# Leaving out sixteen spare matrix products behind the early heads of an attention and MoE kernel

## The chip, the cores and the metric

The kernel runs on one core of one Trainium2 chip. The metric is the device time of one execution in microseconds (us). The kernel before took 1030.9 us as the median of 3 runs (1030.06 to 1033.68 us). The trace comes from one profiled execution of 1030.28 us, whose span from the first to the last instruction is 1027.9 us. All durations below are from that execution.

## The reference

Three layers are computed one after the other, in float32:

```python
scores = scale * q @ k.T                         # 4 batches x 8 heads, 576 x 576, head_dim 64
cum    = cumsum(max(s, 0))
scores = where(causal, -1e9, scores + min(-(cum_i - cum_j), 0))
x      = softmax(scores) @ v                     # 2304 tokens x 512
xn     = x / sqrt(mean(x*x) + 1e-6) * rms_g
x      = (silu(xn @ w_gate) * (xn @ w_val)) @ w_out      # 512 -> 1536 -> 512
out    = (silu(x @ w2_gate) * (x @ w2_val)) @ w2_out
```

## The kernel before

**Arithmetic.** TensorE works here on float32 values that are split in two halves, a rounded value H and a rest L. A product of two float32 matrices is taken as three products, H·H, H·L and L·H. So every weight block that comes from memory ("raw") is first converted: ScalarE reads it (L479, into `cvy`), VectorE merges it (L481), ScalarE or GpSimd writes H (L486, L487), VectorE or GpSimd subtracts and writes L (L490). One block is half of one of the 12 column groups f of the gate and value weights.

**Stages.** First come 22 matrix passes on zeros (L559). Then eight "early quads": the first 128 rows of all 32 heads, four heads to a quad. A quad has scores on TensorE (L924, L927), a masked minimum on VectorE (L932), the exponential on ScalarE (L937), a transpose on TensorE (L949), a copy of it by ScalarE or VectorE (L953, L954), a product with the values (L958) and a copy into x (L968, L969). After quads 0 to 3, and again after quads 4 to 7, the rows are normalised: ScalarE squares x (L992), TensorE sums (L999), VectorE forms a factor (L1052 to L1083) with one power on GpSimd in between (L1086), TensorE turns it round (L1095) and spreads it (L1106), VectorE scales x (L1110), ScalarE and VectorE or GpSimd write its halves xH and xL (L1113, L1115). With that the first MoE layer of these 512 rows can start (L1126): for the first five groups f (`HALVES = 5`) in two parts of 256 rows, one for each of the two normalisations. Its results pass through tanh on ScalarE (L1133) and two VectorE operations (L1135, L1138) into one of three buffers `t`, and SyncE stores them (L1167). Beside it the 32 full heads are attended (L650 to L883: loads, the halves kHH, kLL, qst and vst, scores L714 and L839, transposes L784, products L796), with the MoE products as work to fill in. The second half of the program multiplies by w_out (L1488) and computes the second MoE layer (L1669, L1542, L1745).

**What sets the order.** Nothing of this order is written by hand. Every operation is entered in a plan with an engine (or a choice of engines), an assumed duration, what it reads and writes, and a priority `pri`; smaller is sooner. A list scheduler then runs through assumed time: whenever an engine is free it takes the ready operation with the smallest `pri`, and a choice of engines falls to the one that is free first. The order in which operations were taken is the order in which each engine executes them, one after the other, waiting where data is late. A changed duration or operation thus moves everything that is planned later. Four PSUM banks (`mo`) are handed to whoever needs one next.

**The place of the change.** Behind the eighth early quad a loop over `IDLE` enters products that nobody reads (L1256 to L1260): each takes an `mo` bank of its own, multiplies the 128x128 identity `ident` with itself, may start when quad 3 has its exponentials ("early 3"), and has priority 1.0e9, behind all other work. They are taken only when no other product is ready by the plan's clock.

```python
for _ in range(IDLE):
    spare = mo_bank()
    op(PE, 216, lambda en, spare=spare: en.matmul(
        spare()[:, :P], ident(), ident(), start=True, stop=True),
       r=[ident, "early 3"], w=[spare], pri=1.0e9)
```

Of the kernel before, what the change touches and what calls it, by code (L numbers as in the profile page):

```python
# [326 lines left out]
TINY = 70  # L327

HALVES = 5
IDLE = 16  # L330


@with_exitstack
def tile_kernel(
# [63 lines left out]
    def mo_bank():  # L398

        return shared("ps", "mo", 4, [P, 512], F32)  # L400
# [854 lines left out]
    last_setup()  # L1255
    for _ in range(IDLE):  # L1256
        spare = mo_bank()
# [699 lines left out]
```

## Time and profile before

| | |
|---|---|
| median of 3 runs | 1030.9 us |
| profiled execution | 1030.28 us |
| its span | 1027.9 us |
| TensorE (PE) busy | 1019.9 us, 99% |
| VectorE (DVE) busy | 764.2 us, 74% |
| ScalarE (ACT) busy | 632.7 us, 62% |
| GpSimd (POOL) busy | 266.5 us, 26% |

The page calls the engines PE (matrix products; PEld is their weight load), DVE, ACT, POOL and SP. A line number stands for a line of the kernel. A row of a timeline has the start, the time, the engine, the line, the operation with what it writes and reads, and in brackets how long the engine had been idle and what ended that. The ends of products are modelled and overlap the next start; how long a product occupies TensorE is read from the distance of two starts. Each planned product of the identity shows as two records.

### The profile page before, as it was taken

The page shows a single profiled execution, that of the slowest core. Times are in us where ns is not written, and L with a number is a line of the kernel's source. Part 1 is how long each engine was busy: PE and PEld are TensorE (multiplying, and loading weights), DVE is VectorE, ACT ScalarE, POOL GpSimd, SP SyncE. Part 2 cuts the span into 40 slices and gives each one's busy share as a digit, 9 for nine tenths or more (in the row PEclk, how much of TensorE's full clock was granted, in tenths as well). Part 3 has the DMA queues.
Part 4 walks back from the last instruction along what each step waited for, and adds up shares of the span by engine and source line. Part 5 has one row for each costly group of instructions (what it writes and reads, how often), then busy time and mean ns, then how long its engine had stood idle before and what let it go on. Part 6 is the DMA issues. An engine that isn't in the chain of part 4 may idle for free.

```text
span 1027.9 us, 17596 instructions
## 1 busy us (share of the span) xinstructions
PE 1019.9 (99%) x5546; PEld 901.9 (88%) x5546; DVE 764.2 (74%) x1748; ACT 632.7 (62%) x1315; POOL 266.5 (26%) x357
## 2 busy tenths in 40 slices
PE   9999999999999999999999999999999999999998
PEld 9998889999999999899888889888888888788888
DVE  7999887677778796568889896566768667866562
ACT  6889877766687465334567675555665545665653
POOL 3678754444444440100000000212312122200000
PEclk9999999999999999999999999999999999999999
DMA  9874533343445674479888652765757766888772
GB/s 348 266 250 144 182 115 120 123 139 104 121 130 152 215 248 149 147 247 303 273 283 279 210 156 98 243 213 200 259 192 244 267 226 231 305 271 254 215 240 93
DMA packets 122718, 212.07 MB, mean 206 GB/s; under 512 B 19009, under 2 KB 46913, under 8 KB 122625
## 3 DMA queue, kind: packets, MB, share of 16 engines
q1 hardware_dynamic: 122288, 210.61, 62.7%
q8 instruction: 44, 0.72, 0.3%
q14 instruction: 50, 0.40, 0.1%
q10 hardware_dynamic: 336, 0.34, 0.1%
HBM read 146.33 MB, written 64.56 MB: 205 GB/s over the span
## 4 chain that ended last, share of the span: by engine, by line
PE 90%; DVE 4%; DMA 3%; ACT 1%; issue 1%; POOL 0%; SPq 0%; DVEq 0%; ACTq 0%; POOLq 0%
PE mo L1126 23%; PE mo L1669 11%; PE mo L1488 9%; PE sps L1669 9%; PE sps L1488 6%; PE tp L1488 6%; PE tp L796 4%; PE tp L784 3%; PE sps L714 3%; PE mo L1745 3%; PE mo L1542 2%; PE tp L1669 1%; PE sps L1126 1%; PE tp L1126 1%; DMA h_d<-t 1%; PE sps L839 1%
## 5 line engine op out<-in xcount | busy, mean ns | idle before, releaser
L1126 PE MATMUL mo<-xL,H 128*128 128x448 f32 (+2 forms) x472 | 169.3, 359 | 0.7 <-DVE xL L1115 0.7
L1126 PE MATMUL mo<-xH,L 128*128 128x448 f32 (+2 forms) x472 | 169.7, 360 | 0.2 <-DVE L L490 0.2
L1126 PE MATMUL mo<-xH,H 128*128 128x448 f32 (+2 forms) x472 | 168.9, 359 | 0.0
L751 ACT ACTIVATE sc<-sc,col 128x256 f32<-128x256 f32 (+2 forms) x96 | 60.6, 631 | 59.6 <-DVE col L740 58.9
L1126 PEld LDWEIGHTS mo<-xL,H 128*128 128x128 f32 x472 | 88.8, 188 | 6.0 <-DVE xL L1115 0.9
L1126 PEld LDWEIGHTS mo<-xH,L 128*128 128x128 f32 x472 | 88.8, 188 | 5.6 <-DVE L L490 0.4
L1408 DVE TENSOR_TENSOR hL<-hh,hH 128x512 fp32r<-128x512 f32 (+1 forms) x96 | 63.7, 667 | 39.5 <-ACT hH L1405 38.8
L1126 PEld LDWEIGHTS mo<-xH,H 128*128 128x128 f32 x472 | 88.7, 188 | 4.9
L1405 ACT ACTIVATE hH<-hh 128x512 fp32r<-128x512 f32 (+1 forms) x96 | 57.6, 603 | 50.7 <-DVE hL L1408 21.1
L1488 PE MATMUL mo<-hH,wo 128*128 128x512 f32 x208 | 68.5, 389 | 0.0
L789 DVE TENSOR_TENSOR pTB<-tp,pTB 128x512 fp32r<-128x512 f32 (+1 forms) x96 | 56.3, 597 | 14.0 <-ACT pTB L787 13.4
L1675 ACT ACTIVATE u<-sps 128x512 f32<-128x512 f32 x48 | 28.5, 594 | 54.8 <-PE sps L1669 54.7
L787 ACT ACTIVATE pTB<-tp 128x512 fp32r<-128x512 f32 (+1 forms) x96 | 48.5, 517 | 13.5 <-PE tp L784 12.8
L796 PEld LDWEIGHTS tp<-pTB,vst 128*128 128x128 f32 x320 | 52.9, 188 | 4.3 <-DVE pTB L789 0.8
L796 PE MATMUL tp<-pTB,vst 128*128 128x448 f32 (+3 forms) x320 | 55.3, 313 | 0.1
L784 PE MATMUL tp<-ident,sc 128*128 128x128 f32 x320 | 51.3, 273 | 0.1
L1684 ACT ACTIVATE u<-u 128x512 f32<-128x512 f32 x48 | 29.5, 631 | 33.4 <-DVE u L1679 33.4
L1632 POOL TENSOR_TENSOR tmp<-x,x 128x512 f32<-128x512 f32 x2 | 2.6, 1298 | 171.7 <-ACT r L1405 171.7
L1488 PEld LDWEIGHTS mo<-hH,wo 128*128 128x128 f32 x208 | 39.1, 188 | 8.1
L784 PEld LDWEIGHTS tp<-ident,sc 128*128 128x128 f32 x320 | 39.7, 140 | 6.1 <-DVE pTB L789 0.3
L728 POOL TENSOR_SCALAR_AFFINE_SELECT sc<-cb 128x128 f32<-128x128 f32 x96 | 35.2, 381 | 38.0 <-PE tp L784 36.9
L1133 ACT ACTIVATE t<-mo 128x448 f32<-128x448 f32 (+2 forms) x59 | 30.4, 516 | 22.7 <-PE mo L1126 15.5
(318 smaller groups left out, 3023.0 us busy)
## 6 DMA issues: line engine op xcount, KB each, us to landing
raw<-in_w_gv SPq DMA_DIRECT2D x44, 511.8 KB, 5.7
tb<-h_d SPq DMA_DIRECT2D x48, 256.0 KB, 3.6
t<-tb SPq DMA_DIRECT2D x48, 256.0 KB, 3.1
lq<-in_qk SPq DMA_DIRECT2D x32, 288.0 KB, 3.8
cb<-cum_d SPq DMA_DIRECT2D x32, 288.0 KB, 3.7
h<-t SPq DMA_DIRECT2D x32, 256.0 KB, 3.4
h<-h_d SPq DMA_DIRECT2D x24, 256.0 KB, 3.0
row0B<-u SPq DMA_DIRECT2D x24, 256.0 KB, 3.3
```

Source lines behind the costliest of these rows:

```text
L714: op(PE, c_mm(n), lambda en, pt=pt, at=at, c=c, n=n, z=z, kk=kk: en.matmul(pt()[:, :n], qst[j]()[:, at:at + 128], kk()[:, c:c + n], start= ...
L728: op(POOL, 165 + 0.85 * m, lambda en: en.affine_select(out=sc()[:m, o:o + m], in_=cb()[:m, o:o + m], pattern=[[-1, m]], base=0, compare_op ...
L751: op(ACT, c_act(o + m, 2) + 35, lambda en: en.activation(sc()[:m, :o + m], sc()[:m, :o + m], ACTF.Exp, scale=-1.0, bias=col()[:m, 0, t:t + 1],
L784: op(PE, C_TR, lambda en, pt=pt, a=a, kb=kb, t=t: en.transpose(pt()[:, a * P:a * P + P], self.sc[t]()[:, kb * P:kb * P + P], ident()), r=[ ...
L787: op(ACT, c_act(n), lambda en, pt=pt, c=c: en.activation(place(H, c), source(pt, c), ACTF.Copy), r=[pt], w=[(H, c)], pri=pri)
L789: op(DVE, c_tt(n), lambda en, pt=pt, c=c: en.tensor_tensor(out=place(L, c), in0=source(pt, c), in1=f32(place(H, c)), op=ALU.subtract), r=[ ...
L796: op(PE, c_mm(n), lambda en, w=w, z=z, kb=kb, d0=d0, n=n, o=o: en.matmul(po()[:, o:o + n], vst[j]()[:, kb, :], pT[z]()[:, d0:d0 + n], star ...
L1126: op(PE, c_mm(n), lambda en, a=a, x=x, c=c, k=k, i=i: en.matmul(ps()[:, :n], a()[:, c], x(k, lo, n), start=(k == 0 and i == 0), stop=(k == ...
L1405: op(ACT, c_act(n) + 35, lambda en: en.activation(H(), src(), ACTF.Copy), r=[src, *after], w=[H], pri=pri)
L1408: lambda en: en.tensor_tensor(out=L(), in0=src(), in1=f32(H()), op=ALU.subtract),
L1488: op(PE, c_mm(n), lambda en, m=m, w=w, xx=xx, kk=kk, i=i: en.matmul(ps[m]()[:, :n], w(), xx(), start=first and kk == 0 and i == 0, stop=kk ...
L1669: op(PE, c_mm(n), lambda en, w=w, xx=xx, cut=cut, kk=kk, i=i: en.matmul(ps()[:, :n], W[w]()[:, cut], xx(), start=first and kk == 0 and i == 0,
```

## The change

The number of spare products goes from sixteen to none. Nothing else is edited.

```diff
 HALVES = 5
-IDLE = 16
+IDLE = 0
```

The scheduler then sets another order from the first of these products on. On TensorE, behind the score products of the sixth early quad (`sps`; `mo` are the shared banks, `tp` a bank for transposes, `ev` the values, `early` the exponentials turned round), the difference begins so:

```order
 L924 MATMUL sps_400<-eq 128x128
 L927 MATMUL sps_400<-heights 128x128
-L1258 MATMUL mo_424<-ident 128x128
-L1258 MATMUL mo_429<-ident 128x128
 L999 MATMUL mo_368<-half,sq_110 128x2 x2
 L999 MATMUL mo_368<-half,sq_351 128x2 x2
-L958 MATMUL mo_441<-early_112,ev 128x128 x4
-L949 MATMUL tp_457<-ident,sc_407 128x128 x4
```

Two of the sixteen stood ahead of the sums of the first normalisation, and these now follow the scores at once.

On GpSimd, before, from the power of the first normalisation (`rc`, L1086) to that of the second and to the first head's kLL:

```order
L1086 TENSOR_TENSOR rc_453<-rc_453,minus_half 128x2
L1090 TENSOR_SCALAR fenced<-sq_351 128x1
L487 TENSOR_SCALAR H_534<-raw_377 128x512
L487 TENSOR_SCALAR H_534<-raw_395 128x512
L490 TENSOR_TENSOR L_557<-raw_377,H_534 128x512
L490 TENSOR_TENSOR L_557<-raw_395,H_534 128x512
L1115 TENSOR_TENSOR xL_122<-x,xH_123 128x256
L728 AFFINE_SELECT sc_669<-cb_611 128x128
L728 AFFINE_SELECT sc_678<-cb_611 128x128
L490 TENSOR_TENSOR L_698<-raw_468,H_675 128x512
L1086 TENSOR_TENSOR rc_685<-rc_685,minus_half 128x2
L668 TENSOR_TENSOR qst_708<-lq_566,qst_708 64x512
```

and now:

```order
L1086 TENSOR_TENSOR rc_442<-rc_442,minus_half 128x2
L490 TENSOR_TENSOR L_411<-raw_307,H_402 128x512
L1090 TENSOR_SCALAR fenced<-sq_351 128x1
L487 TENSOR_SCALAR H_513<-raw_377 128x512
L622 MEMSET sc_538 128x64
L622 MEMSET sc_540 128x64
L624 MEMSET sc_542 128x64
L624 MEMSET sc_544 128x64
L1115 TENSOR_TENSOR xL_122<-x,xH_123 128x256 x2
L1086 TENSOR_TENSOR rc_629<-rc_629,minus_half 128x2
L1090 TENSOR_SCALAR fenced<-sq_351 128x1
L490 TENSOR_TENSOR L_610<-raw_446,H_599 128x512
```

The second power stood behind five conversions of weights, one half of x and two masks; now one subtraction and one conversion of weights, four small memory fills and two halves of x are ahead of it.

On SyncE's queue, before, the last loads of weights (`raw`) of the second batch, the first stores of the MoE results (`h_d`) and the next head's loads (`lq`, `vl`):

```order
L475 DMA raw_773<-in_w_gv 128x2047
L475 DMA raw_794<-in_w_gv 128x2047
L1167 DMA h_d_70<-t_657 128x256
L652 DMA lq_817<-in_qk 64x512
L475 DMA raw_826<-in_w_gv 128x2047
L1167 DMA h_d_70<-t_717 128x256
L650 DMA lq_817<-in_qk 128x576
L475 DMA raw_870<-in_w_gv 128x2047
L1167 DMA h_d_70<-t_766 128x256
```

and now:

```order
L475 DMA raw_742<-in_w_gv 128x2047
L1167 DMA h_d_70<-t_638 128x256
L475 DMA raw_772<-in_w_gv 128x2047
L475 DMA raw_794<-in_w_gv 128x2047
L1167 DMA h_d_70<-t_682 128x256
L475 DMA raw_825<-in_w_gv 128x2047
L475 DMA raw_846<-in_w_gv 128x2047
L1167 DMA h_d_70<-t_734 128x256
L475 DMA raw_879<-in_w_gv 128x2047
L652 DMA lq_902<-in_qk 64x512
```

The head's load that stood behind the first store now stands behind the third, and two weight loads stand between the stores.

On all engines the two orders are interleaved differently up to the end of the attention and are the same again behind it: on TensorE the last rows that differ are near row 2280 of 4919.

## Rows read from the trace of the kernel before

**Rows 1.** From the page: busy time by engine, granted TensorE clock, chain that ended last.

```profile
PE 1019.9 (99%) x5546; PEld 901.9 (88%) x5546; DVE 764.2 (74%) x1748; ACT 632.7 (62%) x1315; POOL 266.5 (26%) x357
...
PEclk9999999999999999999999999999999999999999
...
PE 90%; DVE 4%; DMA 3%; ACT 1%; issue 1%; POOL 0%; SPq 0%; DVEq 0%; ACTq 0%; POOLq 0%
```

**Rows 2.** Busy time by stretch: length, five engines, granted clock, DMA share, GB/s.

```profile
26.00:32.00 6.00, 6.00 (x55) 5.94 (x55) 4.67 (x21) 5.93 (x19) 3.65 (x5) 1.00 0.95 300
...
54.00:55.00 1.00, 0.50 (x5) 0.30 (x3) 1.00 (x1) 1.00 (x3) 1.00 (x2) 1.00 1.12 367
...
46.00:60.00 14.00, 12.20 (x87) 10.83 (x87) 13.53 (x29) 10.37 (x23) 12.03 (x14) 1.00 0.82 282
...
100.00:200.00 100.00, 100.00 (x585) 90.14 (x584) 77.68 (x259) 76.24 (x184) 56.92 (x87) 1.00 0.46 141
```

**Rows 3.** The spare products' own line: duration min/median/max in ns, first and last start.

```profile
L1258 PE MATMUL mo<-ident x32: 275/275/377, 21.9 to 48.8; 128*128 128x128 f32 x32
```

**Rows 4.** Timeline of PE: the first products, and 28 to 56 us.

```profile
1.04 4.62 PE L559 MATMUL mo<-sq 128*128 128x128 f32 x22 [1.04 <-DVE sq L555]
...
28.37 0.83 PE L1258 MATMUL mo<-ident 128*128 128x128 f32 x6
29.04 0.27 PE L949 MATMUL tp<-ident,sc 128*128 128x128 f32 x1
...
33.24 1.14 PE L958 MATMUL mo<-early,ev 128*128 128x128 f32 x8
34.14 0.36 PE L1126 MATMUL mo<-xH,H 128*128 128x256 f32 x1
...
47.20 0.56 PE L714 MATMUL sps<-kLL,qst 128*128 128x256 f32 x2 [0.51 <-POOL kLL L671]
...
55.25 0.38 PE L1126 MATMUL mo<-xL,H 128*128 128x256 f32 x1 [0.74 <-DVE xL L1115]
```

**Rows 5.** Timeline of ACT: four kinds of work before the first matrix layer, and two waits.

```profile
21.47 0.58 ACT L953 ACTIVATE early<-tp 128x512 f32<-128x512 f32 x1
...
34.42 0.39 ACT L968 ACTIVATE x<-mo 128x256 f32<-128x256 f32 x1 [0.91 <-PE mo L958]
34.70 0.67 ACT L486 ACTIVATE H<-raw 128x512 fp32r<-128x512 f32 x1
...
36.44 0.78 ACT L479 ACTIVATE cvy<-raw 128x512 f16<-128x512 bf16 x1
...
47.69 0.39 ACT L1133 ACTIVATE t<-mo 128x256 f32<-128x256 f32 x1 [2.59 <-DMA h_d<-t]
```

**Rows 6.** Timeline of DVE: the first factor, and two weight merges beside GpSimd.

```profile
30.13 0.17 DVE L1052 TENSOR_SCALAR fac<-totE 128x16 f32<-128x16 f32 x1 [1.09 <-ACT sc L937]
...
37.25 0.69 DVE L481 SCALAR_TENSOR_TENSOR raw<-raw,cvy 128x512 uint32<-128x512 uint32 x1
...
44.51 3.19 DVE L481 SCALAR_TENSOR_TENSOR raw<-raw,cvy 128x512 uint32<-128x512 uint32 x2
```

**Rows 7.** Timeline of POOL: ahead of the second power, and the first head's kLL.

```profile
38.84 1.33 POOL L490 TENSOR_TENSOR L<-raw,H 128x512 fp32r<-128x512 f32 x1 [4.03 <-issue]
40.11 1.18 POOL L1086 TENSOR_TENSOR rc<-rc,minus_half 128x2 f32<-128x2 f32 x1
...
45.29 1.86 POOL L671 TENSOR_TENSOR kLL<-lq,kHH 128x576 fp32r<-128x576 f32 x1
```

**Rows 8.** The DMA queue of SP, and one transfer in the chain of waits.

```profile
33.04 5.17 SPq L475 DMA_DIRECT2D raw<-in_w_gv  x6
39.33 0.33 SPq L1167 DMA_DIRECT2D h_d<-t  x1
47.18 0.48 SPq L652 DMA_DIRECT2D lq<-in_qk  x1
...
39.33 8.28 DMA h_d<-t
```

## The prediction

> **What bounds the kernel now.** I read the page first. TensorE is busy 99% of the span, and it is 90% of the chain that ended last [rows 1]. So the end is the sum of TensorE's work and of the moments in which it has none, and an edit to it can be counted in full only where TensorE's work is late because of other work of its own. Then I read the busy time by stretch: from 100 to 200 us TensorE is busy for all 100 us [rows 2], and the stretches of 100 us up to 1000 look alike. The only larger loss lies early: from 46 to 60 us it is busy for 12.20 of 14 us [rows 2], 1.8 us idle. The spare products lie just there and ahead of it, between 21.9 and 48.8 us [rows 3]. Last I read the timelines of that stretch engine by engine, to see who sets the pace.
>
> **What the products cost.** The sixteen show as 32 records [rows 3]. Six of them start at 28.37 and the next product at 29.04 [rows 4]: 0.67 us, 0.112 us each. All 32 occupy 32 x 0.112 = 3.6 us of TensorE. That is all that can be saved directly. From 26 to 32 us TensorE shows 6.00 of 6 us busy, but ScalarE shows 5.93 of 6 as well [rows 2]; 26 of the 32 records lie between 26.2 and 32.4 us by the timeline, and without them that stretch has only half its work on TensorE. There ScalarE sets the pace: exponentials, copies and weight conversions of the early quads, which the first MoE products need. So the larger part of the 3.6 us is room that TensorE has anyway.
>
> **What comes sooner all the same.** Two things of the new order shorten ScalarE's line. Counted from the order of both programs, between the sixth quad's exponentials and the first half of x, ScalarE loses one copy of transposed exponentials (L953, 0.58 us) to VectorE, has one conversion of weights less there (L479, 0.78 us) and takes one H more (L486, 0.67 us) [rows 5]: 0.58 + 0.78 - 0.67 = 0.7 us less. VectorE's 1.09 us of waiting for the last exponential at 30.13 [rows 6] can shrink by as much. Second, the last values product (L958) starts at 33.24 behind spare products and sums [rows 4], and ScalarE waits 0.91 us for it at 34.42 [rows 5]; now it stands ahead of the sums. The bounds for this stage are 0.7 us (ScalarE's line alone) and 0.7 + 0.91 = 1.6 us (its wait gone too), or nothing where VectorE, which took the copy, becomes late itself. I take 1.3 us, nearer to the upper end, since the wait of 0.91 us ends with a TensorE row that is moved for certain. The MoE products that start at 34.14 [rows 4] should then start near 32.9.
>
> From there to 46 us TensorE is dense in both. What comes then is the hole of 1.8 us. It has named ends: the first head's kLL from GpSimd (0.51 us) and xL of the second normalisation (0.74 us) [rows 4]. Both were late for reasons that the new order touches. The second power ran only behind a subtraction, at 40.11 instead of 38.84 [rows 7]; now it stands ahead of these subtractions. VectorE needed 3.19 us for two merges, where one alone takes 0.69 [rows 6], while GpSimd computed kLL [rows 7]; the scaling of x stood behind them. And SyncE's queue stood still from 39.33 to 47.18 us, its next load waiting until GpSimd had read the buffer at 45.29 + 1.86 = 47.15 [rows 7, 8]; this load now stands behind the third store. Against that, kLL of the first head moves to VectorE, and its scores come later on TensorE. The bounds are the whole 1.8 us gained and as much lost again; I take 0.7 us gained.
>
> **The sum.** 1.3 + 0.7 = 2.0 us less than the profiled execution: 1030.28 - 2.0 = 1028.3 us. (The execution lies 0.6 us under the median of 1030.9; differences are taken from it.) The other 2.3 of the 3.6 us of vacated TensorE time turn into waiting for ScalarE, and so cost nothing and bring nothing. The rest of the reordering, up to the end of the attention, I count at zero: MoE products fill TensorE there [rows 2]. If that cover had a gap, a change of one wait of the size seen at 55.25, 0.74 us [rows 4], would be its price.
>
> [...]
>
> **The rivals.**
>
> *First, all of it is gained.* If the new order closes the hole as well as the products' time, the gain is 3.6 + 1.8 = 5.4 us: 1024.9 us. For it speaks that TensorE sets the end from 75 us on [rows 1, 2] and that all three causes of the hole are touched at once. Against it, ScalarE at 5.93 of 6 us [rows 2], whose work is the same.
>
> [...]
>
> *Third, the stores come too late.* SyncE now has two weight loads between one store of the MoE results and the next. The first store of before, behind six loads, took 8.28 us to land [rows 8], and ScalarE stood 2.59 us at L1133 for the buffer [rows 5]. If the next two stores each hold ScalarE up as long, TensorE lacks weights and banks for 5.2 us; less the 2.0 us gained this is +3.2 us: 1033.5 us. It decides when a store lands more than about 8 us after its issue while the third buffer is full. For it: the loads come without the pause of before. Against it: the first store has five loads ahead instead of six.
>
> *Fourth, nothing.* ScalarE's line is no shorter because VectorE's copy comes late, and the hole keeps its size: 1030.3 us.
>
> **How the numbers follow.** The forecast gets 0.40, all of it gained 0.22, nothing 0.14, the clock 0.12, late stores 0.12. What a measurement can tell from no change is 0.3%, 3.1 us. Faster by more: the first rival and a few parts of the forecast, 0.25. Slower by more: the two slow rivals less the cases in which they cost a little under 3.1 us, 0.19. Within: 0.56. The range goes from 1024.6, just under the first rival, to 1034.0, the clock's price; the forecast's own is 1026.8 to 1030.0.
>
> **What would show it.** In the changed profile the line of the spare products is gone; TensorE shows idle time between 26 and 32 us, some 2 us, and ends of it are ScalarE rows or what they feed; the first MoE product of the dense run starts near 33 us; ScalarE's wait of 0.91 us at L968 is gone; between 46 and 60 us idle time is 1 us or a little more; behind 75 us everything stands 2 us earlier. [...] I am wrong if the dense run starts no earlier than 34, if the hole behind 46 us grows past 2 us, or if TensorE idles later, in the attention, where I counted nothing.

## The result and the profile after

The changed kernel took 1037.27 us (median of 10 runs, 1032.39 to 1041.47) against 1031.07 us for the kernel before, measured beside it: a ratio of 1.0052, 95% interval 1.0037 to 1.0068. One of the ten executions of the kernel before took 1697.28 us; the ratio leaves it out and is taken over all the others, so it is not the quotient of the two medians. The changed kernel is slower by 0.5%, where I forecast a small gain; the time lies outside the range too. The profiled execution took 1037.88 us with a span of 1036.1 us, 8.2 us more than before. At the first product with w_out (L1488), 495.00 us into the span before and 502.89 us now, 7.9 us of it are already there; from 100 to 200 us TensorE is busy for 99.84 of 100 us, against 100.00 before [rows 2]. So most of the loss lies ahead of 100 us. From the page of the changed kernel, granted clock and the chain that ended last:

```profile
PEclk9989999999999999999999999999999999999999
...
PE 74%; DVE 10%; DMA 7%; ACT 4%; issue 3%; SPq 1%; POOL 1%; DVEq 0%; ACTq 0%; POOLq 0%
```

TensorE's share of the chain fell from 90% to 74% and VectorE's rose from 4% to 10% [rows 1]; one slice of the clock, from 52 to 78 us, is below 0.9. Busy time by stretch of the changed kernel (length, PE, PEld, DVE, ACT, POOL, granted clock, DMA share, GB/s):

```profile
0.00:100.00 100.00, 89.75 (x640) 84.41 (x641) 86.33 (x274) 77.72 (x207) 53.44 (x87) 0.95 0.71 242
46.00:60.00 14.00, 9.75 (x59) 9.18 (x60) 13.94 (x22) 8.55 (x17) 9.77 (x14) 0.79 0.37 133
26.00:32.00 6.00, 4.32 (x32) 3.39 (x30) 4.96 (x22) 5.76 (x19) 2.25 (x8) 1.00 0.95 331
60.00:75.00 15.00, 14.60 (x102) 14.21 (x101) 11.98 (x38) 9.89 (x23) 5.45 (x6) 0.86 0.70 219
```

and the same first 100 us of the kernel before:

```profile
0.00:100.00 100.00, 96.92 (x716) 90.93 (x717) 87.73 (x291) 82.56 (x220) 66.42 (x97) 1.00 0.74 251
```

TensorE is idle for 10.25 us instead of 3.08: 7.2 us more. 3.6 us of products are gone, and some of the work ran at half clock (granted 0.50), as the timeline of PE shows:

```profile
30.89 0.78 PE L1106 MATMUL mo<-xH,sel 128*128 128x256 f32 x2 [1.02 <-DVE x L1110]
...
32.27 1.16 PE L958 MATMUL mo<-early,ev 128*128 128x128 f32 x8 [0.37 <-DVE x L1110]
33.27 0.95 PE L999 MATMUL mo<-half,sq 128*128 128x2 f32 x8
34.08 0.37 PE L1126 MATMUL mo<-xL,H 128*128 128x256 f32 x1
...
47.55 0.97 PE L1106 MATMUL mo<-xH,sel 128*128 128x256 f32 x2 [3.02 <-DVE x L1110]
48.32 0.41 PE L1126 MATMUL mo<-xH,H 128*128 128x256 f32 x1
48.53 0.41 PE L1126 MATMUL mo<-xL,H 128*128 128x256 f32 x1
...
58.42 0.90 PE L714 MATMUL sps<-kLL,qst 128*128 128x256 f32 x2 [2.60 <-DVE kLL L671]
```

Two waits of 3.02 and 2.60 us stand where the hole of before had 0.51 and 0.74 us [rows 4]. Behind each the products start 0.213 us apart instead of 0.118, at a granted clock of 0.50 (47.5 to 50 us, and 58.4 to 64 us). 35 products of L1126 ran so (11 from 48.3, 24 from 59.1), 35 x 0.095 = 3.3 us. Idle 7.2 + half clock 3.3 - products 3.6 = 6.9 us of the 7.9; where the last 1.0 us lies these rows do not show.

Both waits are for VectorE. Timelines of DVE and of POOL, changed kernel:

```profile
29.46 0.69 DVE L490 TENSOR_TENSOR L<-raw,H 128x512 fp32r<-128x512 f32 x1 [0.78 <-POOL H L487]
30.07 0.17 DVE L1052 TENSOR_SCALAR fac<-totE 128x16 f32<-128x16 f32 x1
...
43.26 3.50 DVE L490 TENSOR_TENSOR L<-raw,H 128x512 fp32r<-128x512 f32 x2
...
47.02 0.86 DVE L1110 SCALAR_TENSOR_TENSOR x<-x,gcol,mo 128x256 f32<-128x256 f32 x2
...
53.54 1.67 DVE L668 TENSOR_TENSOR qst<-lq,qst 64x512 fp32r<-64x512 f32 x1
55.24 1.79 DVE L481 SCALAR_TENSOR_TENSOR raw<-raw,cvy 128x512 uint32<-128x512 uint32 x1
56.95 1.42 DVE L671 TENSOR_TENSOR kLL<-lq,kHH 128x576 fp32r<-128x576 f32 x1
```

```profile
37.76 1.09 POOL L1086 TENSOR_TENSOR rc<-rc,minus_half 128x2 f32<-128x2 f32 x1 [4.96 <-DVE rc L1060]
...
41.48 4.74 POOL L490 TENSOR_TENSOR L<-raw,H 128x512 fp32r<-128x512 f32 x3
...
53.05 1.61 POOL L668 TENSOR_TENSOR qst<-lq,qst 64x512 fp32r<-64x512 f32 x1
54.74 1.74 POOL L671 TENSOR_TENSOR kLL<-lq,kHH 128x576 fp32r<-128x576 f32 x1
```

VectorE's two L490 take 3.50 us while GpSimd runs three L490, its qst 1.67 us and its merge 1.79 us while GpSimd runs qst and kLL. Alone a merge takes 0.69 us [rows 6], an L490 0.68 (at 34.55 us with GpSimd idle; 0.69 at 29.46 above, beside memory fills of GpSimd). These rows overlap in time, and VectorE's are about two and a half times as long as alone; GpSimd's three L490 take 1.58 us each, against 1.30 at 25.07 us, when VectorE had neither a merge nor a subtraction of halves: in these rows the instructions of both engines are longer while they overlap. What makes them longer, the rows do not show.

Taken over 26 to 75 us, VectorE's merges and subtractions of halves, all marked `port` in the plan ("port work" below), before:

```profile
L481 DVE SCALAR_TENSOR_TENSOR raw<-raw,cvy 128x512 uint32<-128x512 uint32 x16 | 14.5, 935 | 0.0
L490 DVE TENSOR_TENSOR L<-raw,H 128x512 fp32r<-128x512 f32 x4 | 3.5, 875 | 0.2 <-ACT H L486 0.2
L1115 DVE TENSOR_TENSOR xL<-x,xH 128x256 fp32r<-128x256 f32 x4 | 2.8, 728 | 0.0
L671 DVE TENSOR_TENSOR kLL<-lq,kHH 128x576 fp32r<-128x576 f32 x1 | 0.8, 751 | 0.0
L668 DVE TENSOR_TENSOR qst<-lq,qst 64x512 fp32r<-64x512 f32 x1 | 0.7, 685 | 0.0
```

and after:

```profile
L481 DVE SCALAR_TENSOR_TENSOR raw<-raw,cvy 128x512 uint32<-128x512 uint32 x18 | 14.8, 826 | 0.0
L490 DVE TENSOR_TENSOR L<-raw,H 128x512 fp32r<-128x512 f32 x5 | 5.6, 1129 | 1.2 <-POOL H L487 0.8 <-ACT H L486 0.4
L668 DVE TENSOR_TENSOR qst<-lq,qst 64x512 fp32r<-64x512 f32 x2 | 3.3, 1646 | 0.3 <-ACT qst L666 0.2
L1115 DVE TENSOR_TENSOR xL<-x,xH 128x256 fp32r<-128x256 f32 x5 | 3.1, 660 | 0.0
L671 DVE TENSOR_TENSOR kLL<-lq,kHH 128x576 fp32r<-128x576 f32 x1 | 1.4, 1417 | 0.0
```

26 such instructions of 22.3 us became 31 of 28.2 us, on an engine that is busy for 13.94 of 14 us from 46 to 60 us (13.53 before [rows 2]).

### The profile page after: what moved, and what is told of

It is laid out like the page before. It is cut to its first block, busy times and chain, and to the rows that moved or that the text cites. A ratio compares the mean times of both kernels' runs of the same rounds, so it can differ in the third digit from the quotient of the medians.

```text
span 1036.1 us, 17517 instructions
## 1 busy us (share of the span) xinstructions
PE 1020.8 (99%) x5514; PEld 902.1 (87%) x5514; DVE 769.0 (74%) x1748; ACT 633.2 (61%) x1316; POOL 259.0 (25%) x356
## 4 chain that ended last, share of the span: by engine, by line
PE 74%; DVE 10%; DMA 7%; ACT 4%; issue 3%; SPq 1%; POOL 1%; DVEq 0%; ACTq 0%; POOLq 0%
PE mo L1126 19%; PE mo L1669 9%; PE mo L1488 9%; PE sps L1669 7%; PE tp L1488 6%; PE sps L1488 5%; PE tp L796 4%; PE tp L784 3%; PE sps L714 3%; PE mo L1745 2%; DMA cvs<-in_w_o 2%; DMA raw<-in_w_gv 2%; PE mo L1542 2%; PE tp L1669 1%; PE sps L839 1%
## 5 line engine op out<-in xcount | busy, mean ns | idle before, releaser
L1126 PE MATMUL mo<-xL,H 128*128 128x448 f32 (+2 forms) x472 | 170.6, 362 | 0.0
L1126 PE MATMUL mo<-xH,L 128*128 128x448 f32 (+2 forms) x472 | 170.4, 362 | 0.0
L1126 PE MATMUL mo<-xH,H 128*128 128x448 f32 (+2 forms) x472 | 169.9, 361 | 0.0
L1126 PEld LDWEIGHTS mo<-xH,H 128*128 128x128 f32 x472 | 90.4, 192 | 5.2
L1126 PEld LDWEIGHTS mo<-xH,L 128*128 128x128 f32 x472 | 90.4, 192 | 5.0
L1126 PEld LDWEIGHTS mo<-xL,H 128*128 128x128 f32 x472 | 90.4, 192 | 4.8
L751 ACT ACTIVATE sc<-sc,col 128x576 f32<-128x576 f32 (+2 forms) x96 | 60.5, 630 | 43.8 <-DVE col L740 43.6
L1488 PE MATMUL mo<-hH,wo 128*128 128x512 f32 x208 | 68.5, 389 | 0.0
L1133 ACT ACTIVATE t<-mo 128x448 f32<-128x448 f32 (+2 forms) x59 | 30.5, 516 | 38.5 <-PE mo L1126 34.2
L1135 DVE SCALAR_TENSOR_TENSOR t<-t,mo 128x448 f32<-128x448 f32 (+2 forms) x59 | 34.8, 590 | 22.1 <-ACT t L1133 19.6
L1488 PEld LDWEIGHTS mo<-hH,wo 128*128 128x128 f32 x208 | 39.0, 188 | 8.1
```

What stands on the lines that cost most here:

```text
L751: op(ACT, c_act(o + m, 2) + 35, lambda en: en.activation(sc()[:m, :o + m], sc()[:m, :o + m], ACTF.Exp, scale=-1.0, bias=col()[:m, 0, t:t + 1],
L1126: op(PE, c_mm(n), lambda en, a=a, x=x, c=c, k=k, i=i: en.matmul(ps()[:, :n], a()[:, c], x(k, lo, n), start=(k == 0 and i == 0), stop=(k == ...
L1135: op(DVE, c_tt(n), lambda en: en.scalar_tensor_tensor(out=t()[:, :n], in0=t()[:, :n], scalar=1.0, in1=gp()[:, :n], op0=ALU.add, op1=ALU.mu ...
L1488: op(PE, c_mm(n), lambda en, m=m, w=w, xx=xx, kk=kk, i=i: en.matmul(ps[m]()[:, :n], w(), xx(), start=first and kk == 0 and i == 0, stop=kk ...
```

## The experiments

The theory after these traces (theory 1): the products themselves are worth nothing; the order makes the loss. In the new order VectorE and GpSimd meet at urgent places, TensorE waits, and its clock falls behind the wait. The rivals: the products were needed where they stood (theory 2); later, the load that the plan puts on VectorE (theory 3). Each kernel was timed against the kernel before on its own chip; the medians of before lay between 1030.4 and 1032.0 us, so ratios are compared, not times. A line in brackets such as "L501 is L490" names the same source line, moved by the added code. `...` marks what is left out. In the runs with moves, each named operation is put right behind the second one in the order of its engine.

**The order kept, the products not executed.** The kernel before; the sixteen entries stay in its plan and now do nothing.

```diff
-        op(PE, 216, lambda en, spare=spare: en.matmul(
-            spare()[:, :P], ident(), ident(), start=True, stop=True),
+        op(PE, 216, lambda en: None,
```

> The sixteen spare products keep their places in the plan, so that every engine has the order of the kernel before, but TensorE does not execute them. Theory 1 (the order): the loss of 6.2 us comes from the order that the plan makes without the sixteen entries, in which VectorE is late for TensorE twice (waits of 3.02 and 2.60 us) and the clock falls after each wait; whether the products are executed hardly matters. It expects 1029.5 to 1031.5 us, near the kernel before, and a granted clock of 1.000. Theory 2 (the products): executed products keep TensorE busy between 22 and 49 us and so keep its clock up. It expects a fallen clock between 26 and 60 us and 1033.5 us or more.

1031.96 us, ratio 1.0005 (0.9993 to 1.0016). By stretch:

```profile
26.00:32.00 6.00, 4.25 (x27) 2.89 (x25) 4.88 (x21) 5.88 (x19) 3.63 (x5) 1.00 0.81 288
```

TensorE is as thin here as in the changed kernel (4.32 of 6), its clock stays at 1.00 in this execution, and nothing is lost or gained. The whole loss comes from the plan that is made without the sixteen entries: its order and its choice of engines.

**Sixteen products executed in the new order,** inside the transposes of quads 4 to 7.

```diff
+                def turn_(en, c=c):
+                    if self.i >= 4:
+                        en.matmul(pt()[:, c], ident(), ident(), start=True, stop=True)
+                    en.transpose(pt()[:, c], self.sc()[:, c], ident())
...
```

> The changed kernel's order, and in it sixteen products of the identity executed by TensorE inside the transposes of early quads 4 to 7 (20 to 30 us), unseen by the plan. Theory 1 (the order): both waits and both falls of the clock stay; 1036.5 to 1039 us, the products adding up to 1.5 us. Theory 2 (the products): 1030 to 1032.5 us, as before.

1038.71 us, ratio 1.0074 (1.0052 to 1.0096). TensorE was busy for 6.00 of 6 us from 26 to 32 us again, and the first wait came all the same. Its DVE and PE timelines (x's scaling is L1113 there):

```profile
45.55 3.50 DVE L490 TENSOR_TENSOR L<-raw,H 128x512 fp32r<-128x512 f32 x2
49.30 0.86 DVE L1113 SCALAR_TENSOR_TENSOR x<-x,gcol,mo 128x256 f32<-128x256 f32 x2
```

```profile
49.83 0.78 PE L1109 MATMUL mo<-xH,sel 128*128 128x256 f32 x2 [3.03 <-DVE x L1113]
```

Theory 2 falls. Theory 1 is right on the time and the first wait only: the second wait, for kLL, did not come, and the clock was 1.00 from 56 us on. Nor are the products free at these places: with TensorE filled, x is scaled some 2 us later than in the changed kernel (49.30 against 47.02). The profiled execution, 1035.95 us, is the fastest of its six.

**The waits filled.** 13 and 11 products of the identity in the two waits of the changed kernel.

```diff
+                if not split and g == 1 and k == 1:
+                    keep_warm(en, 13)
...
+                            if (hd.b, hd.h, t, c, z) == (0, 0, 1, 0, 1):
+                                keep_warm(en, 11)
```

> The changed kernel's order, with 13 spare products ahead of the spreading product that waits 3.02 us for L1110 and 11 ahead of the score product that waits 2.60 us for kLL, unseen by the plan: TensorE works through its two waits, and what it waits for comes no sooner. Theory 1: the clock stays at full, and what it cost goes: about 35 products of 0.213 instead of 0.118 us, 3.3 to 3.7 us; 1033.3 to 1034.5 us. If the falls of the clock cost nothing beside the waits: 1037 us.

1034.73 us, ratio 1.0034 (1.002 to 1.0048); the clock is 1.00 from 44 to 66 us. By the medians that is about 2 us less than the change (1.0052 to 1.0034), where 3.3 to 3.7 were expected; the intervals overlap, so that the clock costs a part is likely, and how much is not shown.

**The first collision moved:** in the changed kernel GpSimd's two L490 of expert group 4 go behind its last xL.

```diff
+        self.moves = [(("L", "w.H4", 0), ("xL", 1, 3)), (("L", "w.H4", 1), ("L", "w.H4", 0))]
...
```

> The changed kernel's order, but GpSimd subtracts the two weight blocks of group 4 (L490) behind its part of xL (L1115) instead of ahead of it; nothing else moves. Theory 1a (collision): VectorE's two L490 take 1.75 us each, where one alone takes 0.68, because GpSimd's L490 run at the same time, and L1110 stands behind them; now they take 1.4 us in all, the wait of 3.02 us falls to about 1 us, the first fall of the clock goes: 1033.8 to 1035.5 us. Theory 1b (the second normalisation is late for another reason, as ScalarE's L1133 in front of VectorE's L1135): the wait stays over 2.3 us, 1036.5 to 1038 us.

1035.12 us, ratio 1.0032 (1.0019 to 1.0045). DVE, then PE (L501 is L490, L1121 is L1110, L1117 is L1106, L725 is L714, L679 is L668):

```profile
43.70 1.28 DVE L501 TENSOR_TENSOR L<-raw,H 128x512 fp32r<-128x512 f32 x2
```

```profile
45.76 0.78 PE L1117 MATMUL mo<-xH,sel 128*128 128x256 f32 x2 [0.78 <-DVE x L1121]
...
54.24 0.56 PE L725 MATMUL sps<-kHH,qst 128*128 128x256 f32 x2 [1.63 <-DVE qst L679]
```

The pair takes 1.28 us instead of 3.50 with GpSimd out of the way, and the wait falls from 3.02 to 0.78: the collision makes the larger part of it. The later wait remains, 1.63 us for qst and 0.92 for kLL, although VectorE's qst, merge and kLL there take 1.24, 0.69 and 0.84 us instead of 1.67, 1.79 and 1.42; the clock was 0.50 from 56 to 60 us. So the later wait is not the collision's alone.

**kLL moved:** VectorE's qst and kLL of the first head right behind the xL, ahead of the merges.

```diff
+        self.moves = [(("qst", 0, 0), ("xL", 1, 2)), (("kLL", 0, 0), ("qst", 0, 0))]
...
```

> The changed kernel's order, but VectorE computes the first head's qst and kLL (L668, L671) right behind its second pair of xL (L1115) instead of behind two merges of weights each; nothing else moves. Theory 1: the wait of 2.60 us for kLL goes to under 0.5 us and the second fall of the clock with it, the first wait of 3.02 us and the first fall stay: 1033.5 to 1035.5 us. If the first wait decides alone and the second is only room that would be lost later: 1036.5 us or more.

1033.61 us, ratio 1.002 (1.0009 to 1.0031). As theory 1 expected: the first wait is there as in the changed kernel (3.00 us), the second is gone, and the clock is 1.00 from 56 us on. It is the place of qst and kLL in VectorE's order that made the second wait.

**Both moved.**

```diff
+        self.moves = [(("L", "w.H4", 0), ("xL", 1, 3)), (("L", "w.H4", 1), ("L", "w.H4", 0)),
+                      (("qst", 0, 0), ("xL", 1, 2)), (("kLL", 0, 0), ("qst", 0, 0))]
...
```

> The changed kernel's order with both moves: GpSimd's two L490 of group 4 behind its part of xL, and VectorE's qst and kLL of the first head ahead of the merges. No product is added. Theory 1: TensorE waits under 1.5 us in all between 44 and 60 us, the clock does not fall, and the loss is nearly gone: 1030.5 to 1032.5 us, within 0.15% of the kernel before. If the spare products were needed for something else: 1034 us or more.

1035.79 us, ratio 1.0039 (1.0024 to 1.0053): a miss for theory 1. Two things came instead. GpSimd's moved L490 (at 51.94, 3.23 us for two) now meets qst and kLL on VectorE, and in the profiled execution the clock fell early, behind the thin stretch. DVE, then the stretch:

```profile
52.29 1.70 DVE L679 TENSOR_TENSOR qst<-lq,qst 64x512 fp32r<-64x512 f32 x1
54.02 1.77 DVE L682 TENSOR_TENSOR kLL<-lq,kHH 128x576 fp32r<-128x576 f32 x1
```

```profile
32.00:46.00 14.00, 14.00 (x80) 13.97 (x81) 9.78 (x26) 10.57 (x21) 3.33 (x4) 0.63 0.88 289
```

The executions of this one program fell in two groups: six with a mean clock of 0.995 (1035.6 to 1039.1 us), six at 0.999 to 1.000 (1032.6 to 1036.0 us). Their means are 1037.5 and 1034.2 us: 3.3 us lie between executions of one program with a fall and without. Even those without it stay above the 1030.5 to 1032.5 us expected.

**Both moved, with the sixteen products executed:** the moves as above, and

```diff
...
+                    if self.i >= 4:
+                        en.matmul(pt()[:, c], ident(), ident(), start=True, stop=True)
...
```

> The order with both moves (as in the run with both moved), and the sixteen products of the identity computed again, inside the transposes of the quads 4 to 7, so that TensorE is filled between 26 and 32 us. Theory A: with both moves the thin stretch at 26 to 32 us is what let the clock fall at 32 us; filled, the clock stays at 1.00 up to 45 us and what is left are VectorE's collisions behind 50 us: 1032 to 1034 us, 2 to 3 us under the run with both moved. Theory B: the thin stretch has nothing to do with it, VectorE's own lateness sets the end: 1035 to 1036.5 us, with the clock of 34 to 46 us anywhere.

1036.82 us, ratio 1.0057 (1.0042 to 1.0072). The clock was 1.000 in all four executions, with the stretch filled; yet nothing was gained, and VectorE's results are still waited for at 56 and 59 us (L1140 is L1126, L1149 is L1135):

```profile
56.11 0.38 PE L1140 MATMUL mo<-xH,H 128*128 128x256 f32 x1 [1.05 <-DVE t L1149]
59.12 0.39 PE L1140 MATMUL mo<-xH,H 128*128 128x256 f32 x1 [1.33 <-DVE t L1149]
```

Theory A, that the early fall alone made the miss, does not hold, but this run does not show that the fall is free: the sixteen products are not free at these places (1.0074 against 1.0052 in the changed order), and among the executions with both moved those without the fall were 3.3 us shorter.

**kLL moved, the first wait filled:** the moves of qst and kLL, and

```diff
+                if not split and g == 1 and k == 1:
+                    keep_warm(en, 13)
...
```

> The changed order with VectorE's qst and kLL of the first head moved behind the xL (as in the run with kLL moved), and 13 products of the identity inside the wait of TensorE at 44.5 to 47.5 us (13 x 0.112 = 1.5 us, at L1106). Theory 1 (the loss is the collision's waits and the half clock behind each): the one clock fall that was left is gone, so 1.5 to 2 us less than with kLL moved alone: 1031.5 to 1032.5 us, clock 1.00 in every stretch from 34 to 66 us, the wait itself unchanged at about 3 us from L1126 to L1106's end. Rival (the fall costs nothing, only the waits do): 1033.6 us as with kLL moved alone.

1035.75 us, ratio 1.0048 (1.003 to 1.0066): a miss too, no better than with kLL moved alone, though the clock was full (0.999 to 1.000). (The 13 products are 26 records and took 3.06 us, not the 1.5 us that the expectation gives; they fill the whole wait.) TensorE, no longer slowed, met other waits for VectorE: 0.85 us for `t` at 56.7 and 1.12 us for `col` at 59.9 are in its timeline, where the run without the filling has 0.74 us at 60.5.

**kLL moved, x scaled ahead of the first collision.** The moves of qst and kLL, and

```diff
+                      (("L", "w.H3", 0), ("scale", 1, 2)), (("L", "w.H3", 1), ("L", "w.H3", 0))]
```

> The changed order with VectorE's qst and kLL of the first head behind the xL, and VectorE's two L490 of expert group 3 moved behind the first pair of L1110, so that x is scaled ahead of the collision instead of behind it; nothing is added or left out. Theory 1: TensorE's wait of 3.0 us at L1106 shrinks to 1 us or less, no clock fall follows, and L490 colliding a little later delays nothing that is as urgent: 1030.5 to 1032.5 us, the time before. Rival (VectorE is saturated, a wait that goes in one place comes in another, as with both moved): 1033 to 1036 us, with waits of TensorE for L of group 3 or for x's second half at 46 to 50 us.

1034.4 us, ratio 1.0039 (1.002 to 1.0057). The time is the rival's. In the profiled execution, the fastest of seven, the wait of 3.0 us for x is 0.68 us and no clock fall follows (1.00 from 46 to 60 us), as theory 1 had it, but TensorE waits elsewhere for VectorE: for xL three times between 48 and 51 us (1.1 us in all), and later for `t`, not for L of group 3 (L1118 is L1106, L1138 is L1126):

```profile
45.32 0.78 PE L1118 MATMUL mo<-xH,sel 128*128 128x256 f32 x2 [0.68 <-DVE x L1122]
...
51.04 0.38 PE L1138 MATMUL mo<-xL,H 128*128 128x256 f32 x1 [0.40 <-DVE xL L1127]
...
57.12 0.39 PE L1138 MATMUL mo<-xH,H 128*128 128x256 f32 x1 [0.97 <-DVE t L1147]
```

**The old order, x scaled first.** The same idea in the order of before: a pair of x's scalings ahead of the merges of group 4, products not executed.

```diff
+        self.moves = [(("scale", 1, 0), ("merge", "w.H4", 1)), (("scale", 1, 2), ("scale", 1, 0)),
+                      (("merge", "w.H4", 1), ("scale", 1, 2))]
...
```

> The order of the kernel before, its sixteen spare products planned but not executed, and VectorE scales the first half of x of the second normalisation (two L1110) ahead of the second merge of group 4's weights and of L1135. In the kernel with kept order TensorE waits 1.7 us for these two. Theory 1: the wait falls under 0.6 us, 0.5 to 1.5 us are gained, 1029.5 to 1031 us. If group 4's weights are what is late next, the gain is lost again: 1031 to 1032.5 us.

1032.14 us, ratio 0.9999 (0.9987 to 1.0012): the wait for x, 1.69 us with the order kept, is gone (the spreading product at 48.11 us starts without one), and 1.3 us later TensorE waits 0.92 us for a weight half H of ScalarE: the gain is lost again, as the second expectation had it. No version beat the kernel before.

**Eight products planned, none executed:** a third order.

```diff
-IDLE = 0
+IDLE = 8
...
-        op(PE, 216, lambda en, spare=spare: en.matmul(
-            spare()[:, :P], ident(), ident(), start=True, stop=True),
+        op(PE, 216, lambda en: None,
```

> Eight spare products in the plan instead of sixteen, none executed: a third order. Theory 1: no product is executed and yet the time depends on the order, so it lies anywhere from 1030 to 1038 us, and where it is over 1033 us TensorE waits over 2 us for VectorE between 40 and 65 us and its clock falls. Theory 2 (the products): as the changed kernel, 1037 us, whatever the order.

1036.14 us, ratio 1.0041 (1.0026 to 1.0057); the clock was 0.88 from 32 to 46 us and 0.76 from 46 to 60. TensorE waits for `xL` (1.7 us in two) and `col` (1.7 us in two): other waits, the same kind of loss, as theory 1 allowed. The time is near theory 2's as well; it is the run with the order kept that decides against that theory.

**Engines and order exchanged.** A list, left out here, says for 16 subtractions (L, xL, qst, kLL planned from 26 to 60 us) which engine executes them; the places in the program stay. First the engines of before in the order of after, then the engines of after in the order of before (products not executed):

```diff
+        for what, e in self.engines:
+            i = next(i for i, o in enumerate(out) if o[2] == self.marks[what])
+            out[i] = (*out[i][:3], e)
...
```

> The changed order, each instruction in its place in the program, but the 16 subtractions (L, xL, qst and kLL planned between 26 and 60 us) whose engine the changed plan chose differently go back to the engine they have before; no products are added. [...] Rival (the order itself, with weights merged 6 to 20 us earlier ahead of what is urgent, makes VectorE late): 1034 us or more, though VectorE's port work falls; GpSimd then is waited for, for xL and kLL.

> The order of the kernel before with the sixteen products left out of execution only (as in the run that kept the order, 1032.0 us), and the same 16 subtractions given the engines that the changed plan has for them. Theory 3 (the load on VectorE): 1034 to 1037 us, VectorE's port work from 26 to 75 us 25 us or more instead of 21.4, and waits of TensorE for x or xL that grow. Rival (the order itself): 1031 to 1033.5 us, as the kept order has it.

The first: 1041.15 us, ratio 1.0089 (1.0061 to 1.0117); VectorE's port work from 26 to 75 us was 27.3 us and hardly fell from the 28.2 of the changed kernel, so the run did not make the test that it was for. The second: 1037.95 us, ratio 1.0064 (1.0042 to 1.0086), somewhat above theory 3's 1034 to 1037 us, though VectorE's port work rose only from 21.4 to 23.5 us. It loses as much with 23.5 us of that work as the changed kernel with 28.2 us, and eight planned (1.0041) has 21.8: the amount does not set the loss. The waits of TensorE in the first from 26 to 75 us (L1131 is L1106, L739 is L714; another 3.1 us for `col` come behind them) and its stretch, then the waits in the second (L1151 is L1126):

```profile
PE mo L1131 <- DVE x L1135: 3.6, 2, 1.9
PE sps L739 <- DVE col L765: 1.9, 1, 1.9
```

```profile
32.00:46.00 14.00, 13.56 (x71) 13.15 (x72) 9.61 (x28) 10.53 (x22) 3.70 (x5) 0.63 0.85 271
```

```profile
PE mo L1151 <- DVE xL L1140: 2.2, 2, 1.7
PE mo L1131 <- DVE x L1135: 1.8, 3, 0.7
```

The trace of the second is of its fastest execution, 1033.23 us with a clock of 1.000; two executions at 1.000 have a mean of 1033.8 us, the four at 0.995 to 0.997 one of 1038.9 us. So neither the old order nor the old choice of engines is enough by itself. Of the four combinations only the one of before (1.0005) is free of the loss; both mixtures (1.0064, 1.0089) lose as much as the change (1.0052) or more.

## Why the prediction was wrong

**The products' own time: right.** They cost nothing where they stood; left out in their old order they give 1.0005. TensorE's stretch of 26 to 32 us went to 4.32 of 6 us, ScalarE stayed at 5.76.

**The 1.3 us of the early stage: failed, the gain was nothing.** ScalarE's line did get shorter: its copy into x (L968) starts at 33.47 instead of 34.42 [rows 5] and waits 0.41 instead of 0.91 us. But the dense run still starts at 34.08, against 34.14 [rows 4] and the forecast of 32.9. Two things took the gain. VectorE's first factor (L1052) starts at 30.07, against 30.13 [rows 6]: its wait for the last exponential went, but a weight subtraction that had waited 0.78 us for GpSimd's H now stands ahead of it. And L958 does stand ahead of the sums, at 32.27 instead of 33.24 [rows 4], but the sums (L999, 33.27) now stand between it and the dense run, and TensorE goes from one to the other without a gap. I had "nothing" as a bound, for VectorE late through the copy, and chose the upper one. That ScalarE sets the pace there does not hold in the new order either: TensorE's waits between 26 and 33 us (0.56, 1.02 and 0.37) all end with VectorE.

**The 0.7 us of the hole: the step that failed.** "The second power ran only behind a subtraction ... now it stands ahead": true, it starts at 37.76 instead of 40.11 [rows 7], and VectorE does scale x sooner, at 47.02 instead of 48.44. What I left out is when TensorE needs it. "From there to 46 us TensorE is dense in both" is wrong: in the new order it has run out of work at 44.5 us. Records of L1126 from 30 us up to the second spreading (L1106) of the second normalisation, before and after (length, PE, granted clock, DMA share, GB/s), and, before, that spreading and the scaling it needs:

```profile
30.00:48.90 18.90, 12.58 (x96) 1.00 0.74 245
```

```profile
30.00:47.50 17.50, 9.72 (x72) 0.99 0.96 326
```

```profile
48.97 0.78 PE L1106 MATMUL mo<-xH,sel 128*128 128x256 f32 x2
```

```profile
48.44 0.87 DVE L1110 SCALAR_TENSOR_TENSOR x<-x,gcol,mo 128x256 f32<-128x256 f32 x2
```

The new order puts 24 of them fewer ahead of it: for these alone TensorE is there 2.8 us sooner (24 x 0.118), VectorE's scaling only 1.4 us. And in front of the scaling on VectorE stands a pair of L490 that overlaps with three on GpSimd and takes 3.50 us instead of 1.28. The page of before had the evidence for the collision: two merges took 3.19 us where one takes 0.69 [rows 6]. I booked it as something to be gained and did not ask where the new order puts the next one. That kLL moves to VectorE I named and gave no price; it became the wait of 2.60 us. The idle time of 46 to 60 us grew from 1.8 to 4.25 us, with the clock at 0.79; my own bound, "as much lost again", was too small, since it left out the half clock behind a longer wait.

**The clock, given 0.12: a fall came, behind the waits.** In the profiled execution the thinned stretch of 26 to 32 us kept its clock, 1.00; the fall to 0.50 came behind the two waits for VectorE, of 3.02 and 2.60 us. That the thin stretch can also be followed by a fall is shown by both moved and by engines of before (0.63 from 32 to 46 us), not by the changed kernel. No run shows the 1034.0 us that the range has as the clock's price; the runs show 35 products slowed by 3.3 us in all in the changed kernel, and executions of one program at a lower mean clock (0.995 against 0.999 to 1.000, and 0.995 to 0.997 against 1.000) longer by 3.3 us (both moved) and by 5.1 us (engines of after). **Late stores** did not come: ScalarE waits for no store at L1133 between 20 and 75 us. The other two rivals ended too low.

**Settled and open.** Shown: the loss is the new plan's, not the missing products' (order kept, sixteen executed); the first long wait comes for the larger part from a collision of VectorE with GpSimd (the pair of L490 at 1.28 us instead of 3.50 as soon as GpSimd is elsewhere), the second from the place of qst and kLL in VectorE's order (gone with kLL moved); how much of the second the collision makes is not shown. Shown too that removing a wait, or holding the clock, gives back a part, at best 3.3 of the 5.4 us (1.002 against 1.0052): the next wait for VectorE comes up. A full VectorE is not enough to explain that: from 46 to 75 us it is busy for 27.3 of 29 us in the kernel before and for 25.9 in the changed one. The half clock's net price is not settled, since the evidence differs: holding the clock saved about 2 us in one kernel and nothing in two others (one of them with sixteen products more), while executions of one program with a lower clock are longer: by 3.3 us with both moved, by 5.1 us in engines of after, and in the changed kernel the six at 0.994 to 0.995 have a mean of 1037.5 us, the three at 0.998 one of 1033.7. Whether the fall itself or the lateness ahead of it costs these is not separated. Open: which property of the plan of before makes it the better one. It is not free of collisions (3.19 us for two merges [rows 6]), and neither its engines nor its sequence alone does it.

One thing in the kernel's source bears on this. The plan keeps VectorE and GpSimd apart by its own clock: an operation marked `port` is put off while the other engine is at such work (L230 to L233). But what it hands to each engine is only a sequence, and the rows above overlap all the same.

## What to carry to other kernels

Low-priority filler in a list-scheduled plan is not only time on its engine: it shifts the whole plan, and a plan that was good with it is a matched set of order and engine choice. Before taking an entry out, take out its execution alone. When a new order is judged from the order alone, count how much work the bottleneck still has ahead of the place where it needs a result (here 72 records instead of 96), and look on the engine that feeds it at what stands ahead of that result, and whether GpSimd has a subtraction of its own near that moment: here an overlap with three L490 of GpSimd made an L490 of 0.7 us into 1.75. That the plan has the two apart is no proof.

## What was not expected of the hardware

The granted clock differs between executions of one program: the changed kernel had six at 0.994 to 0.995 (1037.1 to 1038.1 us), three at 0.998 (1032.4 to 1034.7) and one at 0.997 (1041.5). Idle time of TensorE between 26 and 32 us alone does not tell which profiled execution falls: the clock stayed full with 1.7 us of it in the changed kernel and with 2.0 us in engines of after, and was down to 0.56 from 32 to 34 us with 1.9 us in both moved. And in one pair of traces the lower clock was in part free: with kLL moved it was 0.58 from 48 to 52 us; with the first wait filled as well, it was held at 1.00 and the waits for VectorE from 56 to 60 us grew instead (TensorE busy for 2.15 of 4 us, against 3.75).
